# Moving three groups of transfers in a decode-attention backward kernel: early weight loads, an earlier gradient store, and tail stores issued by SP

## The chip, the cores and the metric

The kernel runs on one core of one Trainium2 chip. The time is device microseconds for one execution, and smaller is better. Each engine (PE for matrix products, DVE for vector work, ACT for scalar-scaled copies, POOL, SP) executes its own instructions in order. Transfers between the chip's memory and the core's buffers are issued by an engine (here SP for loads and POOL for nearly all stores) and carried out by the core's 16 DMA engines.

## The reference

One token of width D = 640 goes through a layer norm and then through two branches that are summed: attention over a cached K and V, and a gated MLP.

```python
xn  = layernorm(x)
# A: 32 heads, 8192 cached positions, head width 128
q   = (xn @ wq).reshape(heads)
p   = softmax(q . K^T * 128**-0.5);  o = p . V
# B: F = 1728
h   = silu(xn @ w1) * (xn @ w3)
out = x + o.reshape(1, 4096) @ wo + h @ w2
```

The kernel returns `out` and, for a given gradient of `out`, the gradients of x, K, V, wq, wo, w1, w3 and w2. K and V hold 32 x 8192 x 128 bf16 values each, so each head brings 2 MB (2048 KB) of K and 2 MB of V in, and writes as many bytes of dK and dV out. Both of these gradients are outer products of a vector over positions with a vector over the head width.

## The kernel before

**Start.** SP loads, in this order, the two rows x and the incoming gradient's row (by ACT), three parts of w2, w1, w3, the first wq block (`load_wq(0)`, 1280 KB, eight heads' columns), the first wo block (`load_wo(0)`, 640 KB, four heads' rows), K of head 0, V of head 0 and K of head 1. Then the MLP is computed by the generator `mlp_steps`, whose work is interleaved by `yield` with `prep_steps(0)`, which makes the query and the gradient of o for the first four heads.

The gradients of the MLP's weights overwrite the weights' own tiles and are then stored by POOL. `w2_grad(k)` uses part k of w2 on PE, scales rows on ACT (line 538) and stores the part (line 541). `dx_part` uses w1 or w3 on DVE and PE. `grad_v` writes the gradient over w1 on DVE (line 557). `grad_s` does the same for four fifths of w3 on ACT (line 564).

```python
yield from w2_grad(1)
dx_part(0, w1t, 4, 1)
grad_v(0, w1t, 2, 3)
nc.gpsimd.dma_start(dw1_v, w1t[:])
load_v(1)
load_wq(1)
load_wo(1)
```

The tiles of w1 and w3 (`w1t`, `w3t`) come from the pool that later holds K (three buffers). V of head 1 takes the buffer of w1t, so its load (line 114) waits for the store of w1's gradient to land. K of head 2 takes the buffer of w3t and waits for the store of w3's gradient (line 585) in the same way. The wq and wo blocks have pools of two buffers each; the second blocks find their buffers free from the start.

**The heads.** A loop over heads computes, for head h, the probabilities and gradients and, for head h+1, the scores. Products along the head width are done on DVE (line 348) and summed by PE (line 350). `outer` writes one half of dK or dV of a head into a tile `ot` of 1 MB: 24 of 32 rows on DVE (line 357), 8 on ACT (line 361), and POOL stores it (line 363). There are seven `ot` buffers, so DVE can be at most seven tiles ahead of the stores. The last head's tiles are made by DVE alone. V of head h+2 and K of head h+3 are loaded when their buffers are released.

**Order.** DVE, SP, POOL and ACT run in the order in which the code is written (`tc.manual_schedule`). `steps` holds the next group's preparation and the last group's weight gradients, advanced by `gap()`. `store(dst, src)` issues a weight-gradient store on POOL; with a third argument it goes into the list `late` instead. That list holds the wq gradient of heads 16 to 23 (1280 KB), the wo gradient of heads 24 to 27 (640 KB) and the wq gradient of heads 24 to 27 (640 KB). It is issued on POOL in head 29 = H - 3, between its dV tiles and its dK tiles (lines 635 to 637). After the loop the last head is written out by hand, with the stores of the last wq gradient (line 687) and wo gradient (line 690), both on POOL, and the two small results: SP stores the gradient of x (line 714), ACT the output (line 719).

Of the kernel before, what the change touches and what calls it, by code (L numbers as in the profile page):

```python
# [21 lines left out]
def kernel(  # L22
# [22 lines left out]
    nc = tc.nc  # L45
    H = A_k_cache.shape[1]
# [7 lines left out]
    JH = J // 2  # L54
# [6 lines left out]
    NF, REST = divmod(F, P)  # L61
    NB = NF + 1
    ACT_J = 8
    assert H % GW == 0 and GW % GH == 0 and 0 < REST < P and P % GH == 0
    scale = float(DH) ** -0.5

# [22 lines left out]
    dwo_v = out_5.rearrange("(g p r) c -> g p r c", p=P, r=GH)  # L89
# [7 lines left out]
    with tc.manual_schedule(engines=ORDERED):  # L97
# [8 lines left out]
        def load_k(h):  # L106
            Kt = (vpool if h == 1 else kpool).tile([P, J, DH], BF16, name="Kt", tag="V" if h == 1 else "K")
            nc.sync.dma_start(Kt[:], kc[h])
            kv_tiles[h] = kv_tiles.get(h, [None, None])
            kv_tiles[h][0] = Kt  # L110

        def load_v(h):
            Vt = (kpool if h == 1 else vpool).tile([P, J, DH], BF16, name="Vt", tag="K" if h == 1 else "V")
            nc.sync.dma_start(Vt[:], vc[h])
            kv_tiles[h] = kv_tiles.get(h, [None, None])
            kv_tiles[h][1] = Vt

        grp = {}
        late = []

        def store(dst, src, later=False):
            if later:
                late.append((dst, src))
            else:
                nc.gpsimd.dma_start(dst, src)


        def load_wq(b):
            wq_g = wload.tile([P, NC, GW * DH], BF16, name="wq_g", tag="wq_g")
            nc.sync.dma_start(wq_g[:], wq_v[:, :, b * GW * DH:(b + 1) * GW * DH])  # L130
            for g in range(b * HB, (b + 1) * HB):
                c0 = (g - b * HB) * GH * DH
                grp[g] = dict(wq_all=wq_g, wq=wq_g[:, :, c0:c0 + GH * DH])

        def load_wo(g):
            wo_g = wload.tile([P, GH, D], BF16, name="wo_g", tag="wo_g")
            nc.sync.dma_start(wo_g[:], wo_v[g])
            grp[g]["wo"] = wo_g
# [19 lines left out]
        load_k(0)  # L158
        load_v(0)
        load_k(1)  # L160


        ident_bf = consts.tile([P, P], BF16, name="ident_bf")
# [161 lines left out]
        def new_head(h):  # L325
            st = Head()
            st.h = h
            st.g, st.hh = divmod(h, GH)
            st.G = grp[st.g]
            st.K, st.V = kv_tiles.pop(h)  # L330
            hs[h] = st
            return st
# [20 lines left out]
        def outer(st, vec, w2, wf, dst, h, half):  # L353
            j0 = half * JH
            JD = JH - ACT_J if wf is not None else JH
            ot = opool.tile([P, JH, DH // 2, 2], BF16, name="ot", tag="o")
            nc.vector.tensor_tensor(ot[:, 0:JD],  # L357
                                    vec.rearrange("p (a b) -> p a b", b=2).unsqueeze(1).to_broadcast([P, JD, DH // 2, 2]),
                                    w2[:, j0:j0 + JD, :].unsqueeze(2).to_broadcast([P, JD, DH // 2, 2]), ALU.mult)
            for j in range(JD, JH):  # L360
                nc.scalar.activation(ot[:, j].rearrange("p a b -> p (a b)"), vec, ACTF.Copy,  # L361
                                     scale=wf[:, half, j - JD:j - JD + 1])
            nc.gpsimd.dma_start(dst[h][:, j0:j0 + JH, :], ot[:].rearrange("p j a b -> p j (a b)"))  # L363

        def row_max(st):
            st.S = small.tile([P, J], F32, name="S_sb")
# [15 lines left out]
        def probs(st):  # L382
# [5 lines left out]
            if st.h == H - 1:  # L388
                return
            st.Pf = small.tile([P, 2, ACT_J], F32, name="Pf")  # L390
            nc.scalar.activation(st.Pf[:], st.E[:].rearrange("p (a j) -> p a j", a=2)[:, :, JH - ACT_J:JH],  # L391
                                 ACTF.Copy, scale=rZ[:])
# [17 lines left out]
        def dscores(st):  # L410
# [4 lines left out]
            if st.h < H - 1:  # L415
                st.Uf = small.tile([P, 2, ACT_J], F32, name="Uf")
                nc.vector.tensor_copy(st.Uf[:], st.U2[:, :, 0].rearrange("p (a j) -> p a j", a=2)[:, :, JH - ACT_J:JH])
            for j in range(J):
# [41 lines left out]
        def mlp_steps():  # L460
# [48 lines left out]
            for wi in range(2):  # L509
# [4 lines left out]
                for k, b0 in enumerate(range(0, NB, 4)):  # L514
# [6 lines left out]
                    src = bc_ps[:].rearrange("p b a -> p (b a)")[:, 0:cols]  # L521
# [10 lines left out]
            def w2_grad(k):  # L532
                b0, nb, nfull, w2c = w2_parts[k]
                for b, rows in blocks[b0:b0 + nb]:
                    for ci in range(NC):
                        nc.tensor.matmul(accbank[:, OUT0 + ci:OUT0 + ci + 1], lhsT=w2c[0:rows, b - b0, ci * P:(ci + 1) * P],
                                         rhs=hcol_bf[0:rows, b:b + 1], start=False, stop=True, skip_group_check=True)
                    nc.scalar.activation(w2c[0:rows, b - b0, :], g_bc_bf[0:rows, :], ACTF.Copy, scale=hcol[0:rows, b:b + 1])  # L538
                    if b in (1, 3, 5, 7, 9):
                        yield  # L540
                nc.gpsimd.dma_start(dw2_v[:, b0:b0 + nfull, :], w2c[:, 0:nfull, :])
                if nfull < nb:
                    nc.gpsimd.dma_start(out_8[NF * P:F, :], w2c[0:REST, nfull, :])
# [3 lines left out]
            def dx_part(wi, wt, c0, n):  # L547
                T = tpool.tile([P, n, F], BF16, name="T13", tag="T")
                nc.vector.tensor_tensor(T[:], wt[:, c0:c0 + n, :],
                                        bc_sb[:, wi, :].unsqueeze(1).to_broadcast([P, n, F]), ALU.mult)  # L550
                for i in range(F // DR1):
                    nc.tensor.matmul(dx_ps[:, c0:c0 + n, :], lhsT=ident_bf[:], rhs=T[:, :, DR1 * i:DR1 * (i + 1)],  # L552
                                     start=(wi == 0 and i == 0), stop=(wi == 1 and i == F // DR1 - 1),
                                     skip_group_check=True)

            def grad_v(wi, wt, c0, n):
                nc.vector.tensor_tensor(wt[:, c0:c0 + n].rearrange("p c (a b) -> p c a b", b=2),
                                        bc_sb[:, wi, :].rearrange("p (a b) -> p a b", b=2).unsqueeze(1)
                                        .to_broadcast([P, n, F // 2, 2]),
                                        xn2[:, c0:c0 + n].unsqueeze(2).to_broadcast([P, n, F // 2, 2]), ALU.mult)  # L560
# [6 lines left out]
            yield from w2_grad(0)  # L567
            dx_part(0, w1t, 2, 2)
            grad_v(0, w1t, 0, 2)
            yield from w2_grad(1)  # L570
            dx_part(0, w1t, 4, 1)
            grad_v(0, w1t, 2, 3)
            nc.gpsimd.dma_start(dw1_v, w1t[:])
            load_v(1)
            load_wq(1)
            load_wo(1)
            dx_part(1, w3t, 0, 2)
            yield from w2_grad(2)
            dx_part(1, w3t, 2, 2)
# [13 lines left out]
        def gap():  # L593
            if steps and next(steps[0], "end") == "end":
                steps.pop(0)

        mlp = mlp_steps()
        prep = prep_steps(0)
        next(mlp)
# [16 lines left out]
        for h in range(H - 1):  # L616
            n = new_head(h + 1) if h + 1 < H else None
            c = hs.pop(h)
            g, hh = divmod(h, GH)
            if n:  # L620
                product(n, "S", 0)
            probs(c)
            outer(c, c.do, c.P2, c.Pf, dvc, h, 0)
            if prev:
                keep_dq(prev)
            gap()
            row_dots(c)
            attend(c)
            turn_wq(c)
            if n:  # L630
                product(n, "S", 1)
            outer(c, c.do, c.P2, c.Pf, dvc, h, 1)
            if h + 2 < H:
                load_v(h + 2)
            if h == H - 3:
                for dst, src in late:
                    store(dst, src)
            gap()
            dscores(c)
            outer(c, c.q, c.U2, c.Uf, dkc, h, 0)  # L640
            keep_wq(c)
            if n:
                row_max(n)
                product(n, "DP", 0)
            outer(c, c.q, c.U2, c.Uf, dkc, h, 1)
            if h + 3 < H:
                load_k(h + 3)
            gap()
            if n:
                exps(n)  # L650
                product(n, "DP", 1)
            weights(c)
            gap()
            if hh == 0 and g + 1 < NG:
                if (g + 1) % HB == 0 and g + 1 > HB:
                    load_wq((g + 1) // HB)
                if g:
                    load_wo(g + 1)
            if hh == 1 and g + 1 < NG:
                steps.append(prep_steps(g + 1))  # L660
                gap()
            if hh == 2:
                gap()
            prev = c

        c = hs.pop(H - 1)
        g = c.g
# [19 lines left out]
        store(dwq_v[:, :, g * GH * DH:(g + 1) * GH * DH], c.G["wq"])  # L687
        for r in range(GH):
            nc.scalar.activation(c.G["wo"][:, r, :], g_bc_bf[:], ACTF.Copy, scale=on[:, r:r + 1])
        store(dwo_v[g], c.G["wo"][:])  # L690


        fin = consts.tile([P, NC], F32, name="fin")
# [56 lines left out]
```

## Time and profile before

| | |
|---|---|
| median of 3 runs | 745.63 us (744.89, 745.63, 748.58) |
| profiled execution | 749.68 us, of which its span is 747.5 us |
| moved | 303.71 MB, mean 406 GB/s; half read, half written |
| DVE busy | 632.3 us, 85% of the span |
| PE busy | 548.8 us, 73% |
| ACT busy | 467.7 us, 63% |
| POOL busy | 82.4 us, 11% |
| 128 `ot` stores | 1024 KB each, median 29.1 us from issue to landing |

The profiled execution is one run, with its own time; the median comes from other executions. Times inside a profile are microseconds from the start of the span. "Share" of the DMA engines in a table by windows is the mean busy share of the 16; it can come out a little over 1.

### The profile page before, as it was taken

What the parts mean: (1) busy time and instruction counts of PE and PEld (TensorE: products, weight loads), DVE (VectorE), ACT (ScalarE), POOL (GpSimd) and SP (SyncE); (2) the same over time, 40 slices, a digit from 0 to 9 for tenths busy, and PEclk for the clock granted to TensorE, in tenths of its full rate; (3) what the DMA queues carried; (4) which work ended last, traced back from release to release, by engine and by line L of the source; (5) the groups of instructions that cost most, each with busy time, mean ns of one, the idle gap of its engine ahead of it and who ended that gap; (6) DMA issues with size and microseconds to landing.
All of it is one profiled execution on the core that took longest, in us unless ns stands there. A gap on an engine that the chain in (4) does not pass through costs nothing.

```text
span 747.5 us, 15863 instructions
## 1 busy us (share of the span) xinstructions
PE 548.8 (73%) x6497; PEld 323.7 (43%) x6513; DVE 632.3 (85%) x710; ACT 467.7 (63%) x1385; POOL 82.4 (11%) x156
## 2 busy tenths in 40 slices
PE   5678388878887776886778766886787777777860
PEld 3454145545544433443444334444354444344440
DVE  5589499999997976998798995998898998799991
ACT  2485167796776853795666754787565857677540
POOL 0011011111111100111010110110001111011110
PEclk9597568878877788887988778767796789777775
DMA  9969999999999999999999999999999999999975
GB/s 341 420 248 371 432 379 425 427 422 420 427 429 426 423 417 425 423 426 419 429 429 425 423 419 425 420 425 419 431 426 426 429 403 428 427 429 425 411 309 194
DMA packets 37030, 303.71 MB, mean 406 GB/s; under 512 B 3820, under 2 KB 5550, under 8 KB 11870
## 3 DMA queue, kind: packets, MB, share of 16 engines
q0 software_dynamic: 21728, 151.35, 48.9%
q1 hardware_dynamic: 15218, 151.35, 48.3%
q8 instruction: 51, 0.84, 0.4%
q14 instruction: 21, 0.17, 0.1%
q10 hardware_dynamic: 12, 0.00, 0.0%
HBM read 151.34 MB, written 151.34 MB: 405 GB/s over the span
## 4 chain that ended last, share of the span: by engine, by line
DMA 73%; DVE 17%; PE 5%; ACT 2%; issue 1%; SPq 1%; DVEq 0%; POOLq 0%; ACTq 0%
DMA out_dram<-ot 49%; DMA out_dram<-wo_g 10%; DVE ot L357 7%; DVE T L348 7%; DMA Kt<-in_A_k_cache_dram 6%; DMA wo_g<-in_A_wo_dram 3%; DMA w3t<-in_B_w_dram 2%; DMA out_dram<-w3t 1%; PE psS L350 1%; ACT w3t L564 1%; PE psDP L350 1%; PE dx_ps L552 1%; ACT w2c L538 1%; DVE DP_sb L404 1%; DVE S_sb L367 1%
## 5 line engine op out<-in xcount | busy, mean ns | idle before, releaser
L350 PE MATMUL psDP<-T,ident_bf 128*128 128x512 bf16 x512 | 187.6, 529 | 66.1 <-DVE T L348 66.1
L350 PEld LDWEIGHTS <-ident_bf 128*128 128x128 bf16 x1024 | 120.3, 120 | 230.4 <-issue 177.4
L361 ACT ACTIVATE ot<-qs_g,Uf 128x128 bf16<-128x128 bf16 x496 | 151.5, 389 | 58.2 <-DMA out_dram<-ot 46.0
L361 ACT ACTIVATE ot<-do_g,Pf 128x128 bf16<-128x128 bf16 x496 | 151.5, 389 | 20.4 <-DMA out_dram<-ot 19.6
L348 DVE TENSOR_TENSOR T<-Kt,qs_g 128x4096 bf16<-128x4096 bf16 x64 | 146.4, 2289 | 13.8 <-DMA Kt<-in_A_k_cache_dram 11.1
L350 PE MATMUL psS<-T,ident_bf 128*128 128x512 bf16 x512 | 143.5, 431 | 15.8 <-DVE T L348 15.6
L348 DVE TENSOR_TENSOR T<-Vt,do_g 128x4096 bf16<-128x4096 bf16 x64 | 146.0, 2281 | 0.1
L357 DVE TENSOR_TENSOR ot<-qs_g,U 128x3072 bf16<-128x3072 bf16 (+1 forms) x64 | 113.3, 1770 | 29.7 <-DMA out_dram<-ot 29.5
L363 POOL DMA_DIRECT2D out_dram<-ot x128 | 68.2, 533 | 577.7 <-ACT ot L361 219.6
L357 DVE TENSOR_TENSOR ot<-do_g,P 128x3072 bf16<-128x3072 bf16 (+1 forms) x64 | 113.4, 1772 | 10.6 <-DMA out_dram<-ot 9.8
L419 PEld LDWEIGHTS <-Kt 128*128 128x128 bf16 x2048 | 57.3, 98 | 16.0 <-issue 13.6
L419 PE MATMUL ob<-U,Kt 128*128 128x1 bf16 x2048 | 56.8, 164 | 5.8 <-DVE U L412 5.7
L397 PEld LDWEIGHTS <-Vt 128*128 128x128 bf16 x2048 | 57.2, 97 | 0.0
L397 PE MATMUL ob<-P,Vt 128*128 128x1 bf16 x2048 | 57.0, 163 | 0.0
L391 ACT ACTIVATE Pf<-E,rZ 128x16 f32<-128x16 f32 x31 | 9.6, 308 | 51.9 <-DVE rZ L384 51.9
L253 ACT COPY woT<-ps_t 128x512 bf16<-128x512 bf16 x40 | 23.0, 576 | 29.9 <-PE ps_t L248 29.9
L438 ACT ACTIVATE dq_diag<-ident_bf,odq 128x128 bf16<-128x128 bf16 x32 | 12.7, 398 | 44.9 <-DVE odq L434 44.9
L371 PE MATMUL sm<-ident_f,mrow 128*128 128x128 f32 x64 | 17.8, 366 | 24.7 <-DVE mrow L369 24.3
L380 PEld LDWEIGHTS sm<-rsum,ones_f 128*128 128x128 f32 x64 | 15.6, 270 | 43.7 <-ACT E L379 38.7
L248 PE MATMUL ps_t<-ident_bf,wo_g 128*128 128x128 bf16 x160 | 17.3, 237 | 19.8 <-DMA wo_g<-in_A_wo_dram 18.0
L367 DVE TENSOR_REDUCE S_sb<-psS 128x64 f32<-128x512 f32 x32 | 21.9, 685 | 8.3 <-PE psS L350 8.3
L302 ACT ACTIVATE wo_g<-g_bc_bf,on 128x640 bf16<-128x640 bf16 x28 | 21.6, 817 | 6.6 <-PE accbank L293 5.8
(152 smaller groups left out, 498.7 us busy)
## 6 DMA issues: line engine op xcount, KB each, us to landing
out_dram<-ot POOLq DMA_DIRECT2D x128, 1024.0 KB, 29.1
Kt<-in_A_k_cache_dram SPq DMA_DIRECT2D x32, 2048.0 KB, 18.3
Vt<-in_A_v_cache_dram SPq DMA_DIRECT2D x32, 2048.0 KB, 14.8
wq_g<-in_A_wq_dram SPq DMA_DIRECT2D x4, 1280.0 KB, 21.5
wo_g<-in_A_wo_dram SPq DMA_DIRECT2D x8, 640.0 KB, 9.5
out_dram<-wo_g POOLq DMA_DIRECT2D x8, 640.0 KB, 25.5
out_dram<-wq_g POOLq DMA_DIRECT2D x3, 1280.0 KB, 31.8
w1t<-in_B_w_dram SPq DMA_DIRECT2D x1, 2160.0 KB, 11.7
```

The lines of the kernel that those rows point to most:

```text
L248: nc.tensor.transpose(ps_t[:, hh * DH:(hh + 1) * DH], wo_g[:, hh, ci * P:(ci + 1) * P], ident_bf[:])
L253: nc.scalar.copy(woT[:], ps_t[:])
L302: nc.scalar.activation(wo_g[:, r, :], g_bc_bf[:], ACTF.Copy, scale=on[:, r:r + 1])
L348: nc.vector.tensor_tensor(T[:], src[:, :, ds_], vec[:, ds_].unsqueeze(1).to_broadcast([P, J, DHH]), ALU.mult)
L350: nc.tensor.matmul(ps[:], lhsT=ident_bf[:], rhs=T[:, :, RUN * i:RUN * (i + 1)], start=(half == 0 and i == 0), stop=(half == 1 and i == DHH ...
L357: nc.vector.tensor_tensor(ot[:, 0:JD], vec.rearrange("p (a b) -> p a b", b=2).unsqueeze(1).to_broadcast([P, JD, DH // 2, 2]), w2[:, j0:j0 ...
L361: nc.scalar.activation(ot[:, j].rearrange("p a b -> p (a b)"), vec, ACTF.Copy, scale=wf[:, half, j - JD:j - JD + 1])
L363: nc.gpsimd.dma_start(dst[h][:, j0:j0 + JH, :], ot[:].rearrange("p j a b -> p j (a b)"))
L367: nc.vector.tensor_reduce(st.S[:], st.ps["S"][:], AX.X, ALU.add)
L371: nc.tensor.matmul(st.sm[:, 8:8 + P], lhsT=mrow[:].to_broadcast([P, P]), rhs=ident_f[:], start=True, stop=True, skip_group_check=True)
L397: mm = nc.tensor.matmul(st.ob[:, 0:1], lhsT=st.V[:, j, :], rhs=st.P2[:, j, 0:1], start=(j == 0), stop=(j == J - 1), skip_group_check=True)
L419: nc.tensor.matmul(st.ob[:, 1:2], lhsT=st.K[:, j, :], rhs=st.U2[:, j, 0:1], start=(j == 0), stop=(j == J - 1), skip_group_check=True)
```

## The change

Four moves; no arithmetic changes, and the instructions of PE, DVE and ACT keep their order.

1. `load_wq(1)` and `load_wo(1)` are written directly behind `load_k(1)` at the start. On SP they were behind the load of V of head 1; now they stand ahead of it.
2. `w2_grad(1)` is written behind the store of w1's gradient. On POOL, that store was behind the store of w2's second part; now it stands ahead of it.
3. The list `late` is issued after both dK tiles of head 29 instead of ahead of them. POOL's order is now two `ot` stores, then the three late ones.
4. `TAIL = 2`: the eight `ot` tiles of heads 30 and 31 are stored by SP, and so is the last wo gradient. SP's order at the end is seven `ot` stores, wo, the last `ot`, and the gradient of x. POOL's last instruction is the store of the last wq gradient.

```diff
+    TAIL = 2
...
         load_k(1)
+        load_wq(1)
+        load_wo(1)
...
-            nc.gpsimd.dma_start(dst[h][:, j0:j0 + JH, :], ot[:].rearrange("p j a b -> p j (a b)"))
+            eng = nc.sync if h >= H - TAIL else nc.gpsimd
+            eng.dma_start(dst[h][:, j0:j0 + JH, :], ot[:].rearrange("p j a b -> p j (a b)"))
...
             dx_part(0, w1t, 2, 2)
             grad_v(0, w1t, 0, 2)
-            yield from w2_grad(1)
             dx_part(0, w1t, 4, 1)
             grad_v(0, w1t, 2, 3)
             nc.gpsimd.dma_start(dw1_v, w1t[:])
             load_v(1)
-            load_wq(1)
-            load_wo(1)
+            yield from w2_grad(1)
             dx_part(1, w3t, 0, 2)
...
                 load_v(h + 2)
-            if h == H - 3:
-                for dst, src in late:
-                    store(dst, src)
...
                 load_k(h + 3)
+            if h == H - 3:
+                for dst, src in late:
+                    store(dst, src)
...
-        store(dwo_v[g], c.G["wo"][:])
+        nc.sync.dma_start(dwo_v[g], c.G["wo"][:])
```

## Prediction

> **What bounds the kernel.** The page comes first. DVE is busy 85% of the span, but the chain that ended last belongs to transfers:
>
> ```profile
> DMA  9969999999999999999999999999999999999975
> DMA 73%; DVE 17%; PE 5%; ACT 2%; issue 1%; SPq 1%; DVEq 0%; POOLq 0%; ACTq 0%
> ```
>
> The DMA row has one low digit, the third slice (37 to 56 us), and falls at the end. A table by windows (columns after the width: PE, PEld, DVE, ACT, POOL, clock, DMA share, GB/s) gives sizes:
>
> ```profile
> 39.00:51.00 12.00, 8.99 (x110) 7.88 (x109) 11.29 (x7) 11.11 (x15) 3.47 (x5) 0.94 0.42 149
> 51.00:70.00 19.00, 13.97 (x111) 6.68 (x109) 17.15 (x17) 10.80 (x23) 1.10 (x2) 0.85 0.99 384
> 95.00:120.00 25.00, 22.57 (x288) 13.55 (x288) 24.65 (x29) 17.28 (x58) 3.05 (x6) 0.79 0.97 392
> 120.00:690.00 570.00, 436.96 (x5210) 253.64 (x5219) 504.08 (x542) 386.95 (x1182) 63.95 (x119) 0.80 1.01 424
> 714.00:720.00 6.00, 5.14 (x30) 2.55 (x27) 4.57 (x11) 1.59 (x6) 0.53 (x1) 0.81 0.81 339
> 720.00:723.00 3.00, 2.51 (x87) 2.44 (x88) 3.00 (x3) 0.40 (x1) 0.53 (x1) 1.00 0.12 41
> 723.00:738.00 15.00, 3.69 (x80) 2.99 (x76) 9.11 (x17) 4.19 (x9) 2.97 (x5) 0.50 0.94 369
> 738.00:747.50 9.50, 0.00 (x0) 0.00 (x0) 0.00 (x0) 0.00 (x0) 0.00 (x0) 0.50 0.05 17
> ...
> 741.00:744.00 3.00, 0.00 (x0) 0.00 (x0) 0.00 (x0) 0.00 (x0) 0.00 (x0) 0.50 0.06 25
> 744.00:747.50 3.50, 0.00 (x0) 0.00 (x0) 0.00 (x0) 0.00 (x0) 0.00 (x0) 0.50 0.00 0
> ```
>
> For 570 us all DMA engines are full at 424 GB/s, so a transfer moved inside that stretch gains nothing. Before it lies a hole: 12 x (1 - 0.42) = 7.0 us of idle DMA time between 39 and 51. The end is another stage: DVE waits for a store last at 694.1, then runs 38 us without a transfer in its chain, and the DMA engines run dry from 714 to 723.
>
> The timelines of POOL and SP show what opens the hole (start, duration, line):
>
> ```profile
> 42.05 0.98 POOL L541 DMA_DIRECT2D out_dram<-w2c  x1 [39.66 <-ACT w2c L538]
> 47.62 0.84 POOL L541 DMA_DIRECT2D out_dram<-w2c  x1 [4.59 <-ACT w2c L538]
> 48.45 0.56 POOL L573 DMA_DIRECT2D out_dram<-w1t  x1
> 56.56 0.57 POOL L585 DMA_DIRECT2D out_dram<-w3t  x1 [6.46 <-ACT w3t L564]
> 57.81 0.33 SPq L114 DMA_DIRECT2D Vt<-in_A_v_cache_dram  x1
> 58.18 1.21 SPq L130 DMA_DIRECT2D wq_g<-in_A_wq_dram  x1
> 67.56 0.33 SPq L108 DMA_DIRECT2D Kt<-in_A_k_cache_dram  x1
> ```
>
> The start's loads end near 39.3 (share 0.89 in 38 to 39, 0.12 in 39 to 40). Then SP stands at V of head 1 until w1's store has landed, with the wq load, whose buffer is free, queued behind it. POOL stands at w2's second part, with w1's gradient ready behind it: the DVE timeline ends line 557 at 39.57 + 2.86 = 42.43.
>
> **Edit 1, wq and wo.** No byte is added; 1280 + 640 KB = 1.97 MB move ahead of V. At 424 GB/s they take 4.6 us, from 39.3 to 43.9, in place of idle time. They sit behind K of head 1 in SP's order, so no load of the start is delayed.
>
> **Edit 2, w1's store.** It is issued at 42.05 + 0.98 = 43.03 instead of 48.45, 5.4 us earlier; w2's second part keeps its 47.62, set by ACT. From 39.3 the engines have 1.97 MB, w2's first part 0.98 and w1 2.21: 5.16 MB or 12.2 us, to 51.5. The last engine and the receipt add some 2 us (w1t's landing took 9.2 us, of which 3.4 MB with w2's parts explain 8.1), so V is issued near 53.5 instead of 57.8. w2's remaining parts, 1.23 MB, run to 54.4. The old hole of 7.0 us is full.
>
> **What is late next.** w3's store stays tied to ACT, 56.56. V is issued before it, but bytes follow an issue late: w2's first part took 4.8 us to land, of which 0.98 MB explain 2.3, so start and receipt cost 2.5 together. I give the start 2: V's bytes from 55.5, idle from 54.4. At the latest w3's store ends that idle time at 58, as a POOL store shows bytes 1.5 us after its issue (42.05 to a share of 0.41 in 43 to 44). Then V (2.10 MB) and w3 (2.21 MB) take 10.2 us, to 65.7, and K of head 2 is issued after w3's landing near 66.5, about 1 us earlier than now. The first `ot` store still comes at 66.67, when DVE has computed it. Idle again from 65.7 to about 67.4; at the latest the `ot` store ends that at 68.2. New holes: 1.1 + 1.7 = 2.8 us; at most 3.6 + 2.5 = 6.1, at least about 1, if V and K follow at once.
>
> Behind that the loads are cheaper. K of head 2 had wq and wo and part of V ahead of it and took 23.4 us to land; DVE waited 11.1 us for it (row of line 348, "DMA Kt<-in_A_k_cache_dram: 11.1, 1"). With 1.97 MB less ahead, at half the rate beside the stores, that is up to 9 us earlier, so most of this wait goes. By itself that is worth nothing, as the engines are full from 70 to 95 (share 1.02). But DVE's delay returned as a hole of 25 x (1 - 0.97) = 0.8 us at 95 to 120; that closes. And wq's reads, mixed into 51 to 70, go with 384 GB/s: against 424 this loses 1.8 us in 19; I count 0.6 as won, bounds 0 and 1.8.
>
> Front sum: 7.0 - 2.8 + 0.8 + 0.6 = 5.6 us, ends 0.9 (holes of 6.1 and nothing else won) and 8.6 (holes of 1, wq's 1.8 in full). The saving reaches the end only if DVE can run earlier too. It can: line 357 waited 39.4 us for `ot` buffers in all, 43 times, the last at 694.1.
>
> **Edit 3, late stores.** 2.62 MB, issued at 688.6, 689.2 and 694.4, go behind two `ot` stores, to about 701. POOL was held at 694.38 for 4.43 us by an earlier transfer, so those two `ot` stores go out earlier. Nobody waits for them: the tile that reuses their buffers is written after 722, and the 694.1 wait is for a store issued before the late ones. All of it is still 13 us ahead of the dry stretch, so the bytes to drain before 714 are the same. Zero; bounds -1.4 us (that last wait gone: 1.4 on line 357) and +2.4 (6.2 us of transfer less 6 x 0.19 + 3 x 0.88 = 3.8 idle).
>
> **Edit 4, SP in the tail.** Nine stores move: SP's issue takes 0.33 us, POOL's 0.53, so 0.2 us on the store that restarts the engines at 722.45, and none on those that queue. SP's last load, V of head 31, was issued at 684.35, so no load stands behind a waiting store; only dx_bf does. The bounds are wide: -4.5 us, if the end's straggler goes, and +9, if SP blocks (rivals). I take 0, since the same bytes go over the same 16 engines.
>
> On this the Trainium skill ("DMA: Bandwidth & Descriptors", Rules for kernel authors) speaks against the edit: spreading transfers over SP, ACT and GpSimd does not help bandwidth and saves only issue time. By that, the edit is worth 0.2 us.
>
> **Rivals.**
> *The hole is handed back.* Holes at their upper end, 6.1 us, leave 7.0 - 6.1 + 0.8 = 1.7 us: 743.9. For it: w3's store and the first `ot` store do not move, and both bound the idle time only from behind. Against it: it needs the full 4 us from an SP issue to its bytes, twice.
>
> *The straggler goes.* From 741 to 744 the share is 0.06, one engine of 16, while stores come from POOL alone: some 6 us behind the rest. After the start's loads, from SP alone, 40 to 41 has 0.04, and the others had stopped near 39.3: 1.5 us behind. If SP's stores keep the engines even, 4.5 us more go: 735.5. The skill (same page, Latency and other measured facts) has engines 7 and 15 slower under GpSimd-issued transfers, as a best guess; by it this rival would hold. Against it: only the last 9 MB are moved, and the lag may be older.
>
> *SP blocks: slower.* K of head 1 held SP 4.49 us at its issue, with five loads outstanding. If the last four tiles and wo do so, from the third outstanding on, SP's issues run 722.2, 726.7, 731.2, 735.7, 740.2, and dx_bf at 744.7 lands 8.5 later; 753.2, and 3.5 behind it as now, make a span of 756.7 against 747.5: +9.2, less 5.6 in front +3.6: 749.2. Against it: K was 2 MB behind 7 MB of others, these tiles are 1 MB, 2.5 us apart.
>
> That the edits do not do what they say is excluded: the orders of POOL and SP change as described, and those of PE, DVE and ACT do not.
>
> **Numbers.** The profiled run took 749.68, its span 747.5; 5.6 less is 744.1. It lies 4.05 above the median, so 745.63 - 5.6 = 740.0. Chances: forecast 0.52 (own range 737.5 to 742.5), handed back 0.21, straggler gone 0.15, SP blocks 0.12 (749.2 is its likeliest size; more than half of it I put over 749.4, where the front's gain is also small). The range 735 to 745.5 leaves out the last, the second's top (0.02) and the third's lowest part (0.05). About 0.5%, 3.7 us, is what this measurement can tell from no change; faster by more means under 741.9. Faster: 0.49 + 0.05 + 0.15 = 0.69; slower by more: 0.08; same: 0.23.
>
> **What would show it.** Right: share near 1 from 39 to 54; w1's store at 43.0; V issued at 52 to 55; K of head 2 at 66 to 67 with DVE's wait for it under 3 us; `ot` waits on line 357 up; 714 to 723 still dry; the DVE end 5 to 6 us earlier. Wrong: a share under 0.5 over 5 us or more between 54 and 70; a DVE end that moves less than the holes say; an SP issue of more than 1 us after 700; a drain after the DVE end other than today's 12 us (732.1 to 744).

## Result and the profile after

The changed kernel takes 743.43 us (median of 20 runs, 740.11 to 745.63); the kernel before, run beside it, 749.38 us (20 runs, 744.59 to 750.55). The ratio is 0.9928, with a 95% interval of 0.9912 to 0.9945: 5.4 us (4.1 to 6.6) of 749.4. The forecast was 5.6 us less. Single executions of each kernel spread over some 5 us. The two profiles differ at the start: in the second of the 40 slices the granted PE clock is 0.5 in the profile before and 0.8 in the one after, and the first store of w2 comes at 42.05 before and at 38.12 after. Whether this makes the spread is not shown: a second profile of the changed kernel had the slow start (42.53) and took 742.07 us, this one took 742.77. So the two profiled spans (747.5 and 740.7) can't be set off against each other to the microsecond; the ratio can.

The page of the changed kernel, the DMA slices and the chain that ended last:

```profile
DMA  9999999999999999999999999999999999999982
DMA 71%; DVE 20%; PE 5%; ACT 3%; issue 1%; SPq 0%; DVEq 0%; POOLq 0%
DMA out_dram<-ot 44%; DMA out_dram<-wo_g 11%; DVE T L351 9%; DVE ot L360 7%; DMA out_dram<-wq_g 5%; DMA wo_g<-in_A_wo_dram 5%; DMA wq_g<-in_A_wq_dram 3%; PE psS L353 3%; DMA out_dram<-w3t 2%; DMA Kt<-in_A_k_cache_dram 2%; ACT w2c L542 1%; ACT w3t L568 1%; DVE S_sb L371 1%; PE ob L401 1%; DVE DP_sb L408 1%
```

The low digit of the third slice is gone, and a new item stands in the chain: `out_dram<-wq_g`, 5%. The table by windows (columns as before; the last two are DMA share and GB/s):

```profile
39.00:51.00 12.00, 7.76 (x64) 6.00 (x64) 10.14 (x7) 12.00 (x14) 2.59 (x5) 0.86 1.03 413
...
64.00:66.50 2.50, 1.78 (x49) 1.33 (x47) 2.46 (x5) 2.50 (x10) 0.53 (x1) 1.00 0.49 194
...
95.00:120.00 25.00, 20.61 (x228) 12.12 (x227) 24.54 (x29) 15.05 (x48) 2.67 (x5) 0.91 1.01 430
709.00:713.00 4.00, 3.12 (x100) 2.88 (x100) 3.95 (x6) 0.96 (x2) 0.00 (x0) 1.00 0.52 215
713.00:722.50 9.50, 2.83 (x78) 2.44 (x74) 4.07 (x4) 4.19 (x9) 0.00 (x0) 0.55 0.98 400
722.50:730.75 8.25, 0.00 (x0) 0.00 (x0) 0.87 (x1) 0.00 (x0) 0.00 (x0) 0.50 0.08 33
...
733.00:737.75 4.75, 0.00 (x0) 0.00 (x0) 2.06 (x6) 0.00 (x0) 0.00 (x0) 0.50 0.95 359
```

The hole at 39 to 51 went from a share of 0.42 to 1.03. A new small one stands at 64 to 66.5. The end is another picture than before: for 8 us hardly more than one engine of 16 works (share 0.08; one engine is 0.06), then nothing, then a last burst. The timelines of POOL and SP show the moved transfers:

```profile
40.08 0.55 POOL L576 DMA_DIRECT2D out_dram<-w1t  x1 [0.98 <-DVE w1t L561]
43.37 1.40 POOL L545 DMA_DIRECT2D out_dram<-w2c  x2 [2.74 <-ACT w2c L542]
...
52.43 0.57 POOL L587 DMA_DIRECT2D out_dram<-w3t  x1 [7.09 <-ACT w3t L568]
```

```profile
53.81 0.33 SPq L115 DMA_DIRECT2D Vt<-in_A_v_cache_dram  x1
66.08 0.33 SPq L109 DMA_DIRECT2D Kt<-in_A_k_cache_dram  x1
```

DVE's wait for K of head 2 fell from 11.1 us to 0.4:

```profile
  DMA Kt<-in_A_k_cache_dram: 0.4, 1
```

But DVE's timeline has a wait near its end that the prediction does not know:

```profile
714.82 2.28 DVE L360 TENSOR_TENSOR ot<-qs_g,U 128x4096 bf16<-128x4096 bf16 x1
729.88 1.49 DVE L685 TENSOR_TENSOR wq_g<-dqbc_g,xn 128x2560 bf16<-128x2560 bf16 x1 [12.78 <-DMA out_dram<-wq_g]
...
731.84 2.28 DVE L360 TENSOR_TENSOR ot<-qs_g,U 128x4096 bf16<-128x4096 bf16 x1
```

The last group's wq gradient is written into the same tile, its other half, as the previous group's, and a write to the tile waits until that group's store has landed. This is one of the three late stores. It was issued at 692.44 and landed 37.3 us later.

DVE's last instruction (line 720) starts at 734.90 here and the DMA engines stop 2.6 us after it, at 737.75; before, it started at 732.01 (line 718) and they went on for 12 us. The end of the changed kernel is thus not the end of before, moved forward.

What DVE waited for can be seen by queue. Shares of the 16 engines' time, changed kernel:

| window, us | POOL's queue | SP's queue |
|---|---|---|
| 694 to 698 | 97.5% | 3.9% |
| 702 to 706 | 25.3% | 75.4% |
| 713 to 717 | 4.4% | 98.6% |
| 717 to 722 | 2.3% | 93.4% |
| 724 to 728 | 2.4% | 3.9% |

One engine is 6.25%. From 713 on POOL's queue has less than one engine's time, and from 724 to 728 the two queues together have just that. So nearly all of POOL's late stores was down by 713; what DVE waited for until 729.88 was, by these shares, the rest on one lagging engine, which worked for both queues.

### The profile page after: what moved, and what is told of

The parts are those of the page before. It is cut to its first block, busy times and chain, and to the rows that moved or that the text cites. A ratio compares the mean times of both kernels' runs of the same rounds, so it can differ in the third digit from the quotient of the medians.

```text
span 740.7 us, 15878 instructions
## 1 busy us (share of the span) xinstructions
PE 546.0 (74%) x6513; PEld 322.3 (44%) x6513; DVE 632.3 (85%) x710; ACT 468.0 (63%) x1385; POOL 77.8 (11%) x147
## 4 chain that ended last, share of the span: by engine, by line
DMA 71%; DVE 20%; PE 5%; ACT 3%; issue 1%; SPq 0%; DVEq 0%; POOLq 0%
DMA out_dram<-ot 44%; DMA out_dram<-wo_g 11%; DVE T L351 9%; DVE ot L360 7%; DMA out_dram<-wq_g 5%; DMA wo_g<-in_A_wo_dram 5%; DMA wq_g<-in_A_wq_dram 3%; PE psS L353 3%; DMA out_dram<-w3t 2%; DMA Kt<-in_A_k_cache_dram 2%; ACT w2c L542 1%; ACT w3t L568 1%; DVE S_sb L371 1%; PE ob L401 1%; DVE DP_sb L408 1%
## 5 line engine op out<-in xcount | busy, mean ns | idle before, releaser
L353 PE MATMUL psDP<-T,ident_bf 128*128 128x512 bf16 x512 | 178.5, 509 | 69.5 <-DVE T L351 69.5
L353 PE MATMUL psS<-T,ident_bf 128*128 128x512 bf16 x512 | 149.3, 444 | 4.5 <-DVE T L351 4.4
L367 POOL DMA_DIRECT2D out_dram<-ot x120 | 64.1, 534 | 550.4 <-ACT ot L364 228.6
L383 ACT ACTIVATE E<-S_sb,negM 128x64 f32<-128x64 f32 x32 | 11.0, 343 | 30.0 <-DVE negM L380 30.0
## 6 DMA issues: line engine op xcount, KB each, us to landing
wq_g<-in_A_wq_dram SPq DMA_DIRECT2D x4, 1280.0 KB, 31.7
```

Source lines behind the costliest of these rows:

```text
L353: nc.tensor.matmul(ps[:], lhsT=ident_bf[:], rhs=T[:, :, RUN * i:RUN * (i + 1)], start=(half == 0 and i == 0), stop=(half == 1 and i == DHH ...
L367: eng.dma_start(dst[h][:, j0:j0 + JH, :], ot[:].rearrange("p j a b -> p j (a b)"))
```

## Experiments

Ten other kernels were run, one of them twice, and the changed kernel once more, in three sets on three chips, each beside the kernel before. "Changed" is the kernel above. How far ratios from different sets can be compared shows in the changed kernel itself: 0.9928 above, 0.9952 in the third set, with intervals that overlap.

**The two halves of the change.** First edits 1 and 2 alone (the edit is against the changed kernel):

```diff
-    TAIL = 2
...
-            eng = nc.sync if h >= H - TAIL else nc.gpsimd
-            eng.dma_start(dst[h][:, j0:j0 + JH, :], ot[:].rearrange("p j a b -> p j (a b)"))
+            nc.gpsimd.dma_start(dst[h][:, j0:j0 + JH, :], ot[:].rearrange("p j a b -> p j (a b)"))
...
+            if h == H - 3:
+                for dst, src in late:
+                    store(dst, src)
             gap()
             dscores(c)
...
             if h + 3 < H:
                 load_k(h + 3)
-            if h == H - 3:
-                for dst, src in late:
-                    store(dst, src)
...
-        nc.sync.dma_start(dwo_v[g], c.G["wo"][:])
+        store(dwo_v[g], c.G["wo"][:])
```

> Edits 1 and 2 alone (wq and wo loads early, w1's store ahead of w2's second part); the tail is that of before. Theory A (all of the gain is made at the front, and the tail edits lose some of it: in the changed kernel DVE stands 12.8 us before the last wq gradient, and from DVE's tile of the last dK first half to the last byte it takes 20.7 us against 17.0 before): this kernel is faster than the changed one, ratio to before 0.988 (about -9 us), no wait of DVE for a wq store in the tail. Theory B, as predicted (front 5.6 us, tail 0): ratio 0.9925, equal to the changed kernel. Theory C (the SP stores in the tail bring part of the gain): ratio 0.996 or more.

Measured: ratio 0.9927 (0.9904 to 0.9951), 741.94 us. Theory B holds: the front alone has the whole gain. There is no wait of DVE for a wq store. Its profile has the slow start of before (first w2 store at 42.33), and its span is 741.0 us against 747.5, so the gain is no matter of the start's pace.

Then edits 3 and 4 alone, with the front as before; against the changed kernel:

```diff
-        load_wq(1)
-        load_wo(1)
...
+            yield from w2_grad(1)
...
             load_v(1)
-            yield from w2_grad(1)
+            load_wq(1)
+            load_wo(1)
```

> Edits 3 and 4 alone (late stores behind the dK tiles of head 29, tail stores by SP); the front is that of before. Theory A: +3.7 us, ratio 1.005, with the wait of DVE for the late wq store over 8 us. Theory B: 1.000. Theory C: 0.995 or less, the single engine's tail behind the others gone.

Measured: 1.0014 (0.9986 to 1.0043), 748.43 us. It has the wait, 12.1 us, as theory A said, and yet is no slower than can be told from nothing. Theories A and C both fail on the time: the tail edits are worth about 0 in sum, between -1.0 and +3.2 us by the interval.

**Which tail edit makes the wait.** Edit 3 undone, SP still stores the tail:

```diff
+            if h == H - 3:
+                for dst, src in late:
+                    store(dst, src)
             gap()
             dscores(c)
...
             if h + 3 < H:
                 load_k(h + 3)
-            if h == H - 3:
-                for dst, src in late:
-                    store(dst, src)
```

> Edits 1, 2 and 4, without edit 3: the late stores stay ahead of the dK tiles of head 29. Theory A, if edit 3 makes the wait: the wait of DVE for the wq store is gone (under 1 us) and the ratio to before is 0.988. If instead edit 4 makes it (SP's queue takes the DMA engines from the late stores on POOL's queue, whose packets are smaller), the wait stays over 5 us and the ratio stays at 0.993.

Measured: 0.9954 (0.9930 to 0.9978), 744.05 us. The wait for the wq store is gone, but the time is not better; beside the front alone in the same set (741.94) it is 2 us worse, though the intervals overlap. DVE's waits in the tail of this kernel, with the waiting line, its releaser, total, times and longest:

```profile
DVE ot L360 <- DMA out_dram<-ot: 10.0, 2, 9.8
```

A wait of 9.8 us has come in its place, now for an `ot` buffer. POOL's timeline there shows whose:

```profile
686.13 0.83 POOL L126 DMA_DIRECT2D out_dram<-wq_g  x1 [2.22 <-DMA out_dram<-ot]
692.82 0.55 POOL L367 DMA_DIRECT2D out_dram<-ot  x1 [5.85 <-DMA out_dram<-ot]
695.39 0.53 POOL L367 DMA_DIRECT2D out_dram<-ot  x1 [2.02 <-DMA out_dram<-ot]
```

The last two `ot` stores that POOL still issues are now the ones behind the late stores, and their buffers are needed some thirty microseconds on. The other way round, edit 4 undone and edit 3 kept:

```diff
-            eng = nc.sync if h >= H - TAIL else nc.gpsimd
-            eng.dma_start(dst[h][:, j0:j0 + JH, :], ot[:].rearrange("p j a b -> p j (a b)"))
+            nc.gpsimd.dma_start(dst[h][:, j0:j0 + JH, :], ot[:].rearrange("p j a b -> p j (a b)"))
...
-        nc.sync.dma_start(dwo_v[g], c.G["wo"][:])
+        store(dwo_v[g], c.G["wo"][:])
```

> Edits 1, 2 and 3, without edit 4: the late stores go behind the dK tiles of head 29, and POOL stores the last two heads' tiles as before. If the 12.8 us wait for the late wq store comes from its later place alone (edit 3), it stays over 5 us here. If it comes from SP's stores, which share the DMA engines with POOL's queue (edit 4), it is under 1 us here: everything is one queue in order. In both cases the ratio is near that of the front alone, 0.992 to 0.993, if the tail edits do not move the end.

Measured: 0.9932 (0.9911 to 0.9952), 741.61 us, and this is all that DVE waits for in the tail from 685 on:

```profile
DVE DP_sb L406 <- PE psDP L352: 1.3, 1, 1.3
```

The landing times of the tail's wq stores (minimum, median, maximum; the late 640 KB store is the median here and the maximum of the changed kernel, second line) say the same:

```profile
DMA to landing us min/median/max: 13.2/19.4/21.1
DMA to landing us min/median/max: 3.8/34.6/37.3
```

So the wait takes SP's stores: whatever POOL still has queued when SP begins to store lands late, and it depends on edit 3 only which store that is. In all seven profiles with the tail stored by SP and the late stores on POOL this store took 35.1 to 38.9 us, in the five with POOL alone 19.4 to 23.0. A last form keeps SP's stores and moves the late ones to SP's queue as well:

```diff
                 for dst, src in late:
-                    store(dst, src)
+                    nc.sync.dma_start(dst, src)
```

> The changed kernel with the three late stores issued by SP too, ahead of SP's ot stores, instead of by POOL. If two queues are the cause of the wait (POOL's packets wait behind SP's, and a late store of 37 us follows), the late wq store lands in under 25 us, DVE's wait for it is under 2 us and the ratio is 0.990, like that of the kernel with a tile of its own. If a lagging DMA engine is the cause whatever the queue, the wait stays over 5 us and the ratio at 0.993.

Measured: 0.9916 (0.9887 to 0.9945), 741.10 us. DVE does not wait for a wq store at all; 1.5 us for one `ot` buffer is left. The expectation of a landing under 25 us failed: the 640 KB wq store took 32.2 us on SP's queue too. POOL's `ot` stores of head 29 ran beside it, so this form has two queues at work as well and does not separate the queue from the lagging engine. But SP issued it at 681.7, right behind the load of V of head 31 at 678.2, 11 us sooner than POOL did in the changed kernel (692.44), so that it was down at about 714, before DVE came to its tile at 720.9.

**What the wait costs.** The wait taken away by its cause, the shared tile:

```diff
+        wq_last = opool.tile([P, NC, GH * DH], BF16, name="wq_last", tag="o")
-        nc.vector.tensor_tensor(c.G["wq"].rearrange("p c (a b) -> p c a b", b=2),
+        nc.vector.tensor_tensor(wq_last[:].rearrange("p c (a b) -> p c a b", b=2),
...
-        store(dwq_v[:, :, g * GH * DH:(g + 1) * GH * DH], c.G["wq"])
+        store(dwq_v[:, :, g * GH * DH:(g + 1) * GH * DH], wq_last[:])
```

> The changed kernel with the last wq gradient written to a tile of its own from the pool of ot tiles, so that DVE need not wait for the late wq store of the group that shares its tile. The 12.8 us wait goes (under 1 us left). Theory A: DVE ends 11 to 12 us earlier, and the end follows by 2.5 to 5 us, since the last DMA engine was busy to 730.7 and has two more stores to do (1.7 MB, 4 us): ratio 0.987 to 0.989. Rival: the lagging DMA engine alone sets the end, the gain is under 1 us: ratio 0.992.

Measured: 0.9906 (0.9869 to 0.9943), 740.16 us. The wait is gone, and the gain is between the two expectations' ends. It was run again beside the changed kernel:

> The changed kernel once more, beside the others on the same chip: ratio 0.9928 by its first comparison; DVE's wait for the late wq store 10 to 13 us again if two queues make it, anything if it was chance.

> The changed kernel with a tile of its own once more. If the 12.8 us wait costs the end what the traces say (from 290 MB moved to the last byte 43.2 us with the wait, 41.3 without), it is 2 us under the changed kernel: 0.990 to 0.991. If the wait lies wholly beside the last DMA engine's work, it is equal: 0.993.

Measured in this set: changed kernel 0.9952 (0.9927 to 0.9976), 744.18 us, with a wait of 8.2 us; with the tile of its own 0.9903 (0.9867 to 0.9940), 740.49 us. DVE's timelines, first of the changed kernel, then of the one with the tile:

```profile
718.69 2.28 DVE L360 TENSOR_TENSOR ot<-qs_g,U 128x4096 bf16<-128x4096 bf16 x1
729.15 1.49 DVE L685 TENSOR_TENSOR wq_g<-dqbc_g,xn 128x2560 bf16<-128x2560 bf16 x1 [8.17 <-DMA out_dram<-wq_g]
```

```profile
716.13 2.28 DVE L360 TENSOR_TENSOR ot<-qs_g,U 128x4096 bf16<-128x4096 bf16 x1
718.33 1.48 DVE L686 TENSOR_TENSOR wq_last<-dqbc_g,xn 128x2560 bf16<-128x2560 bf16 x1
...
720.28 2.29 DVE L360 TENSOR_TENSOR ot<-qs_g,U 128x4096 bf16<-128x4096 bf16 x1
```

A wait of 8 to 13 us thus costs some 2 to 4 us at the end. The first pair of ratios gives 1.6 us, but comes from two sets and its intervals overlap; the second, from one set, gives 3.7 us, and single executions hardly overlap (740.43 to 745.61 against 738.99 to 741.47). The rest of it lay beside the DMA engines' work: before, they were busy until 12 us after DVE's last instruction anyway; in the changed kernel they catch up during the wait, and only the last burst of 4.75 us remains.

**The two front edits apart.** Edit 1 alone, against the kernel with edits 1 and 2:

```diff
             grad_v(0, w1t, 0, 2)
+            yield from w2_grad(1)
             dx_part(0, w1t, 4, 1)
             grad_v(0, w1t, 2, 3)
             nc.gpsimd.dma_start(dw1_v, w1t[:])
             load_v(1)
-            yield from w2_grad(1)
```

> Edit 1 alone: wq and wo of the second block loaded behind K of head 1; w1's store stays behind w2's second part. Of the 7.0 us hole, 4.6 us are filled (1.97 MB), and about 2.5 us stay around 47 to 49, where POOL waits for ACT with nothing loading. V of head 1 is issued at 57 to 58 as before, but wq and wo no longer lie behind it. Additive theory (each edit is worth the idle DMA time that it fills): about -4.4 us, ratio 0.994. Rival (V of head 1 is what counts, so without the earlier w1 store nothing is gained): 0.999 to 1.001.

Measured: 0.9924 (0.9895 to 0.9954), 741.32 us: all of the front's gain. Edit 2 alone, against that same kernel with edits 1 and 2:

```diff
         load_k(1)
-        load_wq(1)
-        load_wo(1)
...
             load_v(1)
+            load_wq(1)
+            load_wo(1)
             yield from w2_grad(1)
```

> Edit 2 alone: w1's gradient stored ahead of w2's second part; wq and wo still behind V of head 1. The idle stretch from 39.3 to about 42 or 43.5 stays (about 4 us), the one at 47 to 49 is filled, V is issued near 52. Additive theory: -2.7 to -3 us, ratio 0.996. Rival (V's earlier start is what counts): 0.993, nearly all of the front's gain.

Measured: 0.9987 (0.9966 to 1.0007), 745.94 us: nothing that can be told from no change. The 0.996 of the additive theory lies just outside the interval, the 0.993 of its rival far outside. The windows show where edit 2's gain goes. Edit 1 alone:

```profile
39.00:51.00 12.00, 9.19 (x111) 7.77 (x109) 11.29 (x7) 11.24 (x15) 3.47 (x5) 0.95 0.83 316
51.00:64.00 13.00, 9.39 (x38) 3.84 (x37) 11.33 (x12) 6.09 (x8) 0.57 (x1) 0.87 1.01 382
64.00:80.00 16.00, 13.36 (x158) 7.62 (x157) 15.67 (x17) 10.68 (x36) 2.13 (x4) 0.61 1.01 416
```

Edits 1 and 2 together, a profile whose start ran at the same pace (first w2 store at 42.33; 42.05 with edit 1 alone and before):

```profile
39.00:51.00 12.00, 9.21 (x111) 8.02 (x109) 11.25 (x7) 10.74 (x15) 3.46 (x5) 0.92 1.05 406
51.00:64.00 13.00, 9.40 (x36) 3.95 (x35) 11.16 (x11) 6.12 (x7) 0.57 (x1) 0.87 0.97 333
64.00:80.00 16.00, 13.44 (x158) 7.66 (x157) 15.86 (x17) 10.87 (x36) 2.13 (x4) 0.63 0.97 373
```

In the first window edit 2 adds 12 x (406 - 316) = 1080 KB. In the next two it loses 13 x (382 - 333) + 16 x (416 - 373) = 1325 KB. By 80 us the two stand level: 15.4 MB and 15.2 MB moved since 39, against 13.2 MB before (12 x 149 + 13 x 378 + 16 x 406). The difference to before, about 2.1 MB or 5 us at 424 GB/s, is about the gain of the whole change. The loss is mostly not idle time but low rate: at shares of 0.97 the engines move 333 and 373 GB/s. The trace shows where it starts: V of head 1 is issued at 54.07 instead of 57.70, and its bytes now come beside w3's store from that store's beginning; that store takes 12.8 us to land instead of 10.8, and K of head 2, which waits for it, is issued at 69.87 instead of 67.36. This is read from issue times; no experiment separated it. In edit 2 alone, where V and wq both meet the stores, one window is lower still:

```profile
52.00:56.00 4.00, 1.57 (x8) 0.61 (x6) 2.96 (x4) 0.25 (x1) 0.57 (x1) 0.95 0.89 252
```

**Versions without the wait.** Edit 2 dropped, the tail's wait taken away, once by the tile of its own and once by the late stores on SP:

> Edits 1, 3 and 4 with the last wq gradient in a tile of its own, and without edit 2. If edit 2 is worth nothing on top of edit 1 (the front alone had 0.9927, edit 1 alone 0.9924), this equals the changed kernel with a tile of its own: ratio 0.9905, 2 us under the changed kernel. If edit 2 has some worth that the intervals hid, it is 1 to 2 us slower than that: 0.992 to 0.993.

> Edits 1, 3 and 4 without edit 2, with the late stores issued by SP ahead of the tail's ot stores. No wait over 2 us of DVE for a wq store; equal to the kernel with a tile of its own, 0.990 to 0.991, if edit 2 is worth nothing and the wait was two queues' doing.

Measured: 0.9894 (0.9858 to 0.9931), 740.18 us, and 0.9900 (0.9864 to 0.9936), 740.64 us, beside 744.18 for the changed kernel. Neither waits for a wq store. Together with the second run of the kernel with its own tile (740.49), three kernels without the wait stand 3.5 to 4 us under the changed one; their intervals still touch its lower end (0.9927). Whether they beat the front alone is not shown: only the kernel with its own tile stood in one set with it, and there (740.16 against 741.94) the intervals overlap. Edit 2's absence costs nothing here either.

## Why the prediction was right, and where it was not

*The number.* The forecast of 5.6 us less is met by 5.4. The forecast time of 740.0 is not: it was taken off a median of three executions, 745.63, and twenty gave 749.38. The changed kernel's 743.43 lies outside the narrower range that the prediction gave for its own account (737.5 to 742.5) and beside the 743.9 of its rival; only the ratio tells the two apart.

*The hole.* Right. Its 7.0 us were filled, as the share of 1.03 shows, and V was issued at 54.07 in a run whose start kept the pace of before (53.5 was worked out). The front measured 0.9927, 5.5 us of 747.9, against a sum of 5.6.

*Edit 1 against edit 2.* The sum gave 4.6 us of the filled hole to edit 1, the remaining 2.4 to edit 2, and charged 2.8 us of new holes to both. Read that way edit 2 nets to nothing, which is what was measured; but the prediction never drew that line. The loss itself was put in the wrong form. Forecast were idle engines at 54 to 55 and 66 to 67; found was, in the changed kernel, one hole of 2.5 us at half share (64 to 66.5, 1.3 us in all), and in the front alone, with the pace of before, a dip to 0.60 in 67 to 68. The rest was lost at nearly full shares and low rates (from 51 to 80 us, 13 x (378 - 333) + 16 x (406 - 373) = 1113 KB less than before, 2.6 us at 424 GB/s), which the prediction valued the other way, as 0.6 us to be won. That this comes near the 2.8 us charged for holes is luck.

*K of head 2.* DVE's wait for it went from 11.1 to 0.4 us (under 3 was given). The hole at 95 to 120 closed: 1.01 and 430 GB/s against 0.97 and 392. K's issue at 66 to 67 was wrong. It was worked out from the slow start of before, and with that start it came at 69.87 (front alone) and 69.91 (changed kernel, second profile), as w3's store took longer to land (12.8 us in the front alone) than the 10 us of the sum; the 66.08 of the first profile goes with a start 4 us faster.

*Edit 3, "nobody waits for them".* Wrong. The prediction followed the `ot` buffers and not the third store's own tile. The trace before could have shown it: line 683 writes `wq_g`, the name of the late store's source. There the store was down in time, 20.5 us after its issue at 694.38 and 12 us before DVE came to the tile, so the wait did not show. It takes edit 4 as well: without it nobody waits, as the prediction says. The bound given for edit 3, +2.4 us, covers only the lowest part of what the wait costs (2 to 4 us).

*Edit 4, 0 us.* Right within the intervals, but not for the reason given: DVE lost 8 to 13 us to a wait, and most of that was won back because the DMA engines had less left to do behind DVE's end. The rule of the Trainium skill ("DMA: Bandwidth & Descriptors", Rules for kernel authors) that spreading transfers over more issuing engines brings no bandwidth agrees with the pair 0.9928 (all four edits) and 0.9932 (without edit 4). What is missed by "the same bytes go over the same 16 engines" is which bytes come first.

*The signs for the end.* Three failed in the changed kernel. DVE's end did not come 5 to 6 us earlier but 2.9 us later, the drain behind it was 2.6 us and not 12, and the `ot` waits fell from 39.4 to 31.7 us. In the front alone DVE's end came 6.4 us earlier (line 718 at 725.61) and the engines went on for some 12 us, to 737.4: there the front's saving reached the end as the prediction says. The `ot` waits did not rise there either (38.8 us).

*Rivals.* Handed back: true of edit 2, not of the whole. Straggler gone: false; with SP's stores one engine was nearly alone from 722.5 to 730.75, longer than before, and where the wait is gone it stands at the end again (share 0.06 to 0.09 from 730 to 738 in the last kernel above). The same page, under Latency and other measured facts, calls some DMA engines slower and ties it, as a best guess, to GpSimd-issued transfers. Nothing here supports that as the cause, and nothing excludes it: in that last kernel what was left from 731 to 738 was all of SP's queue, but no run shows which engine it was or when it fell behind. SP blocks: false; every `ot` issue on SP took 0.33 to 0.35 us.

## What to carry to other kernels

When the DMA engines are full, look for the stretch where they are not, and ask which transfer has its buffer free and merely stands behind one that has not: moving that one (edit 1) was the whole gain. Starting the waiting transfer itself earlier (edit 2) can be worth nothing; here, by the issue times, it met other traffic that gates the next one. Before delaying a store or splitting stores over two queues, list every later write to the stored tile, halves included: here a store that nobody had waited for held DVE for 8 to 13 us.

## What was not expected of the hardware

A full DMA share is not a full rate: in the profile of edit 2 alone 4 us went at 252 GB/s with a share of 0.89, and the front's windows had 333 GB/s at 0.97, while the long middle stretch has 424. Why V's load and w3's store beside each other went so much slower than the loads and stores of the middle was not separated.

With two queues storing, what was already queued on POOL landed late: the 640 KB late wq store took 37.3 us from issue, against 20.5 in the kernel before and 19.4 in the one with edits 1 to 3, which store from POOL alone. By the shares above nearly all of it was down by 713, and one engine that worked for both queues had the rest until 729.8. An engine that lags by 6 to 8 us shows at the end of the kernel before, too; why one of the 16 lags stays open.
